# A retention and mixture-of-experts kernel: the first expert's rows turned set by set into four banks, and two output tiles run together by kind of product

## The chip, the cores and the metric

The kernel runs on one core of a Trainium2 chip. The metric is the time of one execution on the device in microseconds (us); 409.28 us is the median of three executions before the change.

## The reference

Retention with a decaying state for 4 batches of 8 heads over 768 steps, then a mixture of 8 experts over the 3072 rows that come out, each row going to the one expert with the largest logit.

```python
for t in range(S):                        # attention part, B=4 H=8 S=768 D=64
    state = gamma * state + k[t] v[t]^T
    y[t] = scale * q[t] state
x = y.transpose(0, 2, 1, 3).reshape(3072, 512)
logits = normalized(x) @ normalized(expert_emb).T / tau
expert_idx = argmax(logits, axis=1)       # gate_w: softmax probability of that expert
for e in range(8):
    mask = expert_idx == e
    h = np.maximum(x[mask] @ w1[e], 0.0)  # 512 -> 1024
    out[mask] = gate_w[mask, None] * (h @ w2[e])
```

## The kernel before

**Two parts.** The attention runs as 12 blocks of 256 steps (the loop over `m`, 0 to 11). Each block gives two banks of PSUM, `py0` and `py1`, which ScalarE copies to `yT` (function `take`, lines 460 and 463). From `yT` come the rows, written to the table `xd` in memory, and the logits: TensorE multiplies (`logits_products`, line 488), VectorE turns the result (`logits_rows`), a further product sums it (`sums`, line 506), VectorE picks the expert (`choose`), and `count` (lines 533 to 537) with `ranks` gives every row its slot in a table, into which GpSimd scatters the row's number (`place`). This goes by groups of blocks; the last two groups are block 10 with its predecessor (`done` in the last pass) and block 11 alone (`g`).

**Experts.** Weights come in pieces of 512 KB. Every piece is split in a high part (`whi`, a rounded copy by ScalarE, line 219) and a low part (`wlo`, the difference, VectorE, line 224), and so are the activations (`xh` and `xl`, `hh` and `hl`). A product of two such numbers is three TensorE products: high by high, high weight by low activation, low weight by high activation. One output tile of the first layer (`first_layer`, line 237) is 4 steps over the inner dimension (`kt`) with three products each, 12 in all, summed in one PSUM bank. There are eight such tiles (`ft`); `hidden` takes a finished one through the ReLU (ScalarE, line 243) and makes the low part (VectorE, line 246).

**The first expert starts early.** 288 of its rows are gathered into `xge` while the attention's last blocks still run, as two sets of 128 rows and one of 32 (`EROWS`). TensorE transposes them (`turn_rows`, line 613): one bank for each `kt`, its three sets one behind the other. ScalarE casts each bank to `xh` (line 620) and VectorE subtracts to `xl` (line 621). The first expert's products are then handed out by `run(n)`, which issues the next n products, so that the logits' steps of the last block stand between them.

**Order.** Instructions of each engine execute in the order in which the program issues them, since the schedule is set by hand for all five engines. PSUM has eight banks. Four (`b0` to `b3`) are taken in turn by `pt_()`; accumulators of the experts go through `py0`, `py1`, `pst0`, `pst1`, `b0`, `b1` (`acc_()`). A bank's next user waits until its last reader is done. So the first two accumulators of the first expert, `py0` and `py1`, wait for `take` of block 11.

Of the kernel before, what the change touches and what calls it, by code (L numbers as in the profile page):

```python
# [11 lines left out]
F32 = mybir.dt.float32  # L12
# [5 lines left out]
ALU = mybir.AluOpType  # L18
# [6 lines left out]
P = 128  # L25
# [9 lines left out]
KT = DM // P  # L35
# [70 lines left out]
def retention_moe(ctx: ExitStack, tc: tile.TileContext, q, k, v, emb, tau, w1, w2, const, const16, out):  # L106
# [45 lines left out]
    def bank(tag, bufs=1):  # L152
        return ps_.tile([P, 512], F32, name=tag, bufs=bufs)
# [5 lines left out]
    def pt_():  # L159
        npt[0] += 1  # L160
        return bank(turn_of[npt[0] % len(turn_of)])
# [291 lines left out]
    def intra(m, u):  # L453
        for j in range(KT):
            for a in range(2):
                y_product(m, u, j, a, vs[m][:, u, 2 * j + a], pms[a, u][:, j])
# [72 lines left out]
    def count(g):  # L529
        r = span(g)  # L530
        nb = r.stop - r.start
        pr = pt_()
        nc.tensor.matmul(pr[:, :nb * NE], ones, cum[:, r.start:r.start + 1].broadcast_to([P, nb, NE]), start=True,
                         stop=False, skip_group_check=True)
        nc.tensor.matmul(pr[:, :nb * NE], tri, oh[:, r], start=False, stop=False, skip_group_check=True)
        for i in range(1, nb):
            nc.tensor.matmul(pr[:, i * NE:nb * NE], ones, oh[:, r.start:r.stop - i], start=False, stop=(i == nb - 1),
                             skip_group_check=True)
        return pr
# [9 lines left out]
    def ranks(g, pr):  # L549
        r = span(g)  # L550
        nb = r.stop - r.start
        rs = ap_.tile([P, nb, NE], F32, name="rs", bufs=1)
        nc.vector.tensor_tensor(out=rs, in0=pr[:, :nb * NE].rearrange("p (c e) -> p c e", e=NE), in1=oh[:, r], op=ALU.mult)
        yield
        nc.vector.tensor_reduce(out=rank[:, r], in_=rs, axis=AX.X, op=ALU.add)
        yield
        nc.vector.scalar_tensor_tensor(out=sloti[:, r], in0=wmn[:, r], scalar=16.0 * STRIDE, in1=rank[:, r],  # L557
                                       op0=ALU.mult, op1=ALU.add)
        yield
# [13 lines left out]
    def run_all(*gs):  # L573
        gs = list(gs)
        while gs:
            gs = [g for g in gs if next(g, gs) is not gs]
# [30 lines left out]
        tokens(P, 0, slice(0, 3))  # L607
        return i

    def turn_rows(xr, jn, kt, ps=None):  # L610
        ps = pt_() if ps is None else ps
        for c, (j, n) in enumerate(jn):
            nc.tensor.transpose(ps[:, c * P:c * P + n], xr[:n, j, kt * P:(kt + 1) * P], ident[:n, :n])
        return ps

    def rows_T(xr, jn, kt, at, ps=None):

        ps = turn_rows(xr, jn, kt) if ps is None else ps
        w = at.stop - at.start
        nc.scalar.copy(out=xh0[:, kt, at], in_=ps[:, :w])  # L620
        nc.vector.tensor_tensor(out=xl0[:, kt, at], in0=ps[:, :w], in1=xh0[:, kt, at].bitcast(F32), op=ALU.subtract)  # L621

    def expert_emb():
        em = ap_.tile([NE, DM], F32, name="parts")
# [136 lines left out]
    for m in range(NM):  # L761
        nxt = m + 1 < NM
        done = last_of.get(m - 1)
        if waiting is not None:
            pr = count(waiting)
            run_all(ranks(waiting, pr))
            if span(waiting).stop == NBE:
                pad()
            ready += range(span(waiting).start, span(waiting).stop)
        py_of(m)  # L770
        if m == NM - 2:
            first = [split_cast(), split_cast()]

        for u in range(2):
            o = masks(scores(m, u), u)
            if u == 0:
                i = o[0]
        n = 2 if m < 7 else 3 if m < 8 else 4
        if m == NM - 2:
            place(ready)  # L780
            ready = []
        if m == 0:
            for j in (*load_q(2), load_k(2)):
                after(j, i)
            nc.sync.dma_start(out=cst2, in_=const[:, _C1:])
            nc.sync.dma_start(out=tri, in_=const16)

        if m + 2 < NM:
            for s in range(2):
                after(scale_k(m + 2, s), i)  # L790
            for s in range(2):
                after(scale_q(m + 2, s), i)
        if m == 2:
            nc.gpsimd.tensor_copy(out=zt[:, :, :2].bitcast(I32), in_=C("ids").rearrange("p (n o) -> p n o", o=2))
        place(ready[:n])
        del ready[:n]
        if m == NM - 3:
            load_piece()
            load_piece()
        if m == NM - 2:  # L800
            early_slots()
            gathered = early_gather()
        if m and m + 3 < NM:
            for j in load_q(m + 3):
                after(j, i)
        if m == 0:
            state(0)
            state_copy(0)
            state_sums(0)
            intra(0, 0)  # L810
            intra(0, 1)
            transpose_k(1, 0)
            i = transpose_k(1, 1)
            after(load_v(2), i)
            inter(0)
            transpose_q(1, 0)
            i = transpose_q(1, 1)
            for j in (*load_q(3), load_k(3), load_v(3)):
                after(j, i)
            state(1)  # L820
            state_copy(1)
            state_sums(1)
        else:
            inter(m)
            if nxt:
                i = state(m + 1)
                state_copy(m + 1)
                if m + 3 < NM:
                    after(load_k(m + 3), i)
            if m == 2:  # L830
                after(nc.sync.dma_start(
                    out=tbl.rearrange("(e s) c -> e (s c)", e=NE)[:, :FILL * SW].rearrange("e (p x) -> e p x", p=P // NE),
                    in_=none), i)
            for i in () if m < 3 else (0, 1, 2) if m == 3 else (m - 1,):
                logits_rows(i, logits_products(i))
            if nxt:
                state_sums(m + 1)
                spread_v(m, 1, nc.vector.tensor_copy)
                transpose_k(m + 1, 0)
                transpose_q(m + 1, 0)  # L840
                i = transpose_q(m + 1, 1)
                if m + 3 < NM:
                    after(load_v(m + 3), i)
                transpose_k(m + 1, 1)
                if m == NM - 2:
                    spread_v(m + 1, 0)
                if m == NM - 3:
                    z = sums(done)
                    run_all(choose(done, z))
                    run_all(add_counts(done))  # L850
                rows(m - 1, gathered if m == NM - 2 else None)
                if m == NM - 2:
                    for low in first:
                        low()
                    load_piece(gathered)
                    load_piece(gathered)
                if done is not None and m != NM - 3:
                    z = sums(done)
                    run_all(choose(done, z))
                    run_all(add_counts(done))  # L860
                intra(m, 0)
                intra(m, 1)
            else:
                intra(m, 0)
                z = sums(done)
                run_all(choose(done, z))
                run_all(add_counts(done))
                for low in lows:
                    low()
                intra(m, 1)  # L870
                pr = count(done)
                ps = [turn_rows(xge, EROWS, kt, bank(f"pst{kt}")) for kt in range(2)]
                run_all(ranks(done, pr))
                place(range(span(done).start, span(done).stop))
        waiting = done
        take(m)
        if m < NM - 2:
            spread_v(m + 1, 0)
        if m == NM - 2:
            spread_v(m + 1, 1)  # L880
            lows = [split_cast(), split_cast()]
        if m < 3:
            next(emb_steps)
        if m == NM - 1:
            for kt in range(KT):
                rows_T(xge, EROWS, kt, slice(0, EARLY), ps[kt] if kt < 2 else None)

        for _ in range(LOADS.count(m)):
            load_piece()
# [6 lines left out]
    held = []  # L896

    def products():
        for ft in range(FT):
            acc = acc_()  # L900
            yield from first_layer(0, ft, acc, xh0, xl0, early)
            hidden(ft, acc, hh0, hl0, early, held if ft < 2 else None)

    todo = products()

# [7 lines left out]
        nc.sync.dma_start(out=tb[:, e], in_=tbl[ds(expert[e] * STRIDE, NG * P), :2 + NE].rearrange("(j p) o -> p j o", p=P))  # L913

    m, g = NM - 1, len(GROUPS) - 1
    pl = logits_products(m)
    logits_rows(m, pl)
    rows(m - 1)
    load_piece()
    load_piece()  # L920
    run(11)
    low = split_cast()
    z = sums(g)
    run_all(choose(g, z))
# [435 lines left out]
```

## Time and profile before

| what | value |
|---|---|
| median of 3 executions | 409.28 us (408.39 to 411.97) |
| the profiled execution | 409.33 us, of which the span from first to last instruction is 407.6 us |
| TensorE busy | 392.3 us, 96% of the span |
| VectorE, ScalarE, GpSimd busy | 254.2 us, 213.5 us, 154.8 us |
| hardware DMA queue q1 | 74.60 MB, 64.5% of the 16 engines' span |
| mean granted TensorE clock | 0.986 of full speed |

Busy shares are means over the whole span. The place of the change is a stretch of some 10 us, from about 121 to 131 us, between the last attention block and the first expert; there the order of the engines' instructions and what each waits for are to be read, not the shares.

### The profile page before, as it was taken

Reading aid. Unit: us, or ns where it says so; the run is one execution under the profiler, and the core shown is the slowest. Engines: PE = TensorE matmul, PEld = TensorE weight load, DVE = VectorE, ACT = ScalarE, POOL = GpSimd, SP = SyncE. Lnnn points to the kernel's source line nnn. Section 1 sums busy time; section 2 is a strip of 40 time slices with the busy share of each in tenths; the row PEclk is TensorE's granted clock in tenths of the full one; section 3 lists DMA queues with packets and bytes.
Section 4 is the critical chain, followed back from the end, with each engine's and each line's share of the span. In section 5 each row is a group of like instructions: output and inputs, shape, how many; then the busy total and the mean of one; then the engine's idle time right before and its main releaser. Section 6 shows DMA issues by size and latency. Waiting matters only on the chain.

```text
span 407.6 us, 9526 instructions
## 1 busy us (share of the span) xinstructions
PE 392.3 (96%) x3646; PEld 359.1 (88%) x3646; DVE 254.2 (62%) x539; ACT 213.5 (52%) x378; POOL 154.8 (38%) x170
## 2 busy tenths in 40 slices
PE   7999999999899999999999999999999999999993
PEld 3998788878687998899999999999889889999972
DVE  5496877767489847871963676396266465586400
ACT  4565566545484627543745644565475365563410
POOL 2666477676333270701631330261274062000040
PEclk9999999999799999999999999999999999999997
DMA  8998979888437978879596896888969958934121
GB/s 233 266 291 255 270 218 261 238 220 245 112 81 189 277 233 198 282 222 276 187 297 166 254 301 197 233 280 248 257 242 329 206 183 247 247 127 126 32 98 53
DMA packets 88479, 88.39 MB, mean 217 GB/s; under 512 B 10808, under 2 KB 67000, under 8 KB 88424
## 3 DMA queue, kind: packets, MB, share of 16 engines
q1 hardware_dynamic: 83176, 74.60, 64.5%
q0 software_dynamic: 5072, 13.03, 9.4%
q8 instruction: 30, 0.49, 0.5%
q14 instruction: 25, 0.20, 0.1%
q10 hardware_dynamic: 176, 0.07, 0.1%
HBM read 65.01 MB, written 18.79 MB: 206 GB/s over the span
## 4 chain that ended last, share of the span: by engine, by line
PE 76%; DVE 6%; issue 6%; DMA 5%; SPq 4%; POOL 1%; ACT 1%; POOLq 0%; DVEq 0%; ACTq 0%
PE pst L237 11%; PE b L237 9%; PE py L237 8%; PE py L1030 8%; PE b L1030 6%; PE pst L1030 6%; PE py L444 5%; PE b L381 5%; PE b L1078 4%; PE py L1078 4%; PE pst L415 2%; SPq L1042 2%; PE b L350 2%; DMA tbl<-parts 2%; DVE x L468 2%
## 5 line engine op out<-in xcount | busy, mean ns | idle before, releaser
L224 DVE TENSOR_TENSOR wlo<-raw,whi 128x1024 fp32r<-128x1024 f32 x64 | 77.8, 1219 | 21.0 <-ACT whi L219 13.6
L1060 POOL DMA_INDIRECT out_dram<-og,si x28 | 30.4, 1086 | 125.1 <-ACT og L1053 88.7
L219 ACT CAST whi<-raw 128x1024 fp32r<-128x1024 f32 x64 | 66.2, 1044 | 2.1 <-DMA raw<-in_moe_w_dram 2.1
L1011 DVE STREAM_TRANSPOSE xt<-xg 128x384 f32<-128x384 f32 (+1 forms) x28 | 15.7, 579 | 34.1 <-DMA xg<-xs 33.9
L596 POOL DMA_INDIRECT xr<-xd,gi x24 | 29.9, 1244 | 17.2 <-ACT sq L278 9.9
L401 DVE TENSOR_TENSOR pm<-b,mask 128x512 f32<-128x512 f32 x48 | 29.8, 681 | 9.1 <-PE b L381 9.1
L344 POOL TENSOR_TENSOR hl<-wlo,cst 128x512 f32<-128x512 f32 x22 | 22.7, 1051 | 32.9 <-DMA wlo<-in_k_dram 20.9
L237 PE MATMUL pst<-xl,whi 128*128 128x380 f32 (+7 forms) x96 | 32.1, 335 | 0.2 <-issue 0.2
L237 PE MATMUL pst<-xh,whi 128*128 128x380 f32 (+7 forms) x96 | 32.0, 334 | 0.0
L237 PE MATMUL pst<-xh,wlo 128*128 128x380 f32 (+7 forms) x96 | 32.0, 333 | 0.0
L566 POOL DMA_INDIRECT tbl<-zt,sloti x24 | 24.4, 1018 | 19.2 <-DVE sloti L557 8.9
L381 PE MATMUL b<-qT,kT 64*128 64x128 f32 x384 | 27.9, 283 | 2.9 <-issue 2.0
L1012 ACT CAST xh<-xt 128x408 fp32r<-128x408 f32 (+6 forms) x28 | 14.3, 510 | 28.4 <-DVE xt L1011 27.4
L381 PEld LDWEIGHTS b<-qT,kT 64*128 64x128 f32 x384 | 24.0, 187 | 5.6 <-issue 3.8
L237 PE MATMUL py<-xl,whi 128*128 128x288 f32 (+7 forms) x80 | 26.3, 328 | 0.5 <-DVE xl L621 0.5
L237 PE MATMUL b<-xh,whi 128*128 128x408 f32 (+7 forms) x80 | 26.7, 334 | 0.0
L237 PE MATMUL b<-xl,whi 128*128 128x408 f32 (+7 forms) x80 | 26.7, 333 | 0.0
L237 PE MATMUL b<-xh,wlo 128*128 128x408 f32 (+7 forms) x80 | 26.6, 332 | 0.0
L237 PE MATMUL py<-xh,whi 128*128 128x288 f32 (+7 forms) x80 | 26.3, 329 | 0.0
L237 PE MATMUL py<-xh,wlo 128*128 128x288 f32 (+7 forms) x80 | 26.2, 328 | 0.0
L444 PE MATMUL py<-pm,vs 128*64 128x128 f32 x384 | 24.3, 277 | 0.3 <-DVE vs L394 0.3
L243 ACT ACTIVATE hh<-pst 128x380 fp32r<-128x380 f32 (+7 forms) x24 | 11.6, 484 | 23.8 <-PE pst L237 23.1
(222 smaller groups left out, 1036.5 us busy)
## 6 DMA issues: line engine op xcount, KB each, us to landing
raw<-in_moe_w_dram SPq DMA_DIRECT2D x60, 512.0 KB
whi<-in_q_dram SPq DMA_DIRECT2D x24, 256.0 KB
xd<-x SPq DMA_DIRECT2D x48, 128.0 KB
wlo<-in_k_dram SPq DMA_DIRECT2D x11, 512.0 KB
xs<-xr SPq DMA_DIRECT2D x6, 768.0 KB
whi<-in_v_dram SPq DMA_DIRECT2D x6, 512.0 KB
wlo<-in_v_dram SPq DMA_DIRECT2D x6, 512.0 KB
xg<-xs SPq DMA_DIRECT2D x16, 192.0 KB
```

What stands on the lines that cost most here:

```text
L219: nc.scalar.copy(out=hv, in_=rv)
L224: eng.tensor_tensor(out=lv, in0=rv, in1=hv.bitcast(F32), op=ALU.subtract)
L237: nc.tensor.matmul(acc[:, :w], a[:, f], x[:, kt, cols], start=(n == 0), stop=(n == 3 * KT - 1))
L344: return eng.tensor_tensor(out=ks_r[:, m % 3, s, h], in0=kin[m % 3][:, h, s], in1=w[:, h], op=ALU.mult)
L381: nc.tensor.matmul(psc[a][:, j], kTs[m][a * D:(a + 1) * D, j, u].rearrange("p s c -> p (s c)"), q_cols(m, a, j, u), start=True, stop=True, ...
L401: o.append(nc.vector.tensor_tensor(out=pm, in0=psc[a], in1=w, op=ALU.mult))
L444: nc.tensor.matmul(pys[m][u][o * D:(o + 1) * D, j], lhsT, rhs, start=first, stop=True, skip_group_check=True)
L566: i = nc.gpsimd.indirect_dma_start(out=tbl[:, :], out_offset=bass.IndirectOffsetOnAxis(ap=sloti[:, n:n + 1], axis=0), in_=zt[:, n], in_off ...
L596: return nc.gpsimd.indirect_dma_start(out=xr[:n, j, :], out_offset=None, in_=xd[:rows_, :], in_offset=bass.IndirectOffsetOnAxis(ap=gi[:n, ...
L1030: nc.tensor.matmul(acc[:, :c], a[:, f], x[:, kt, :c], start=(n == 0), stop=(n == 3 * FT - 1))
L1060: i = nc.gpsimd.indirect_dma_start(out=out[:, :], out_offset=bass.IndirectOffsetOnAxis(ap=si[:n, e, j:j + 1], axis=0), in_=og[:n, j, :], i ...
L1078: nc.tensor.matmul(acc[:s, :], x[:, kt, at], a, start=(n == 0), stop=(n == 3 * FT - 1))
```

## The change

- The rows are turned set by set: the first 128 rows into all four banks (`pst0`, `pst1` and two of `b0` to `b3`), then the second 128, then the last 32. The transposes now stand ahead of `count`, where before they stood behind it.
- The four casts to `xh` (`rows_high`) are issued ahead of `take` of block 11, where before they came behind it. The four subtractions (`rows_low`) come ahead of the second of two weight splits, of `ranks` and of `place`.
- The first two output tiles open together, in two accumulators: for each kind of product (high by high, then low activations, then low weights) and each `kt`, one product for each of the two tiles.
- The first 12 products stand ahead of `logits_products` of block 11, 6 more ahead of the next split and `sums`, where before 11 came between these two and none ahead.

```diff
-    def turn_rows(xr, jn, kt, ps=None):
-        ps = pt_() if ps is None else ps
+    def turn_rows(xr, jn, ps):
         for c, (j, n) in enumerate(jn):
-            nc.tensor.transpose(ps[:, c * P:c * P + n], xr[:n, j, kt * P:(kt + 1) * P], ident[:n, :n])
-        return ps
-
-    def rows_T(xr, jn, kt, at, ps=None):
-
-        ps = turn_rows(xr, jn, kt) if ps is None else ps
-        w = at.stop - at.start
-        nc.scalar.copy(out=xh0[:, kt, at], in_=ps[:, :w])
-        nc.vector.tensor_tensor(out=xl0[:, kt, at], in0=ps[:, :w], in1=xh0[:, kt, at].bitcast(F32), op=ALU.subtract)
+            for kt in range(KT):
+                nc.tensor.transpose(ps[kt][:, c * P:c * P + n], xr[:n, j, kt * P:(kt + 1) * P], ident[:n, :n])
+
+    def rows_high(kt, at, ps):
+        nc.scalar.copy(out=xh0[:, kt, at], in_=ps[:, at])
+
+    def rows_low(kt, at, ps):
+        nc.vector.tensor_tensor(out=xl0[:, kt, at], in0=ps[:, at], in1=xh0[:, kt, at].bitcast(F32), op=ALU.subtract)
...
                 run_all(add_counts(done))
-                for low in lows:
-                    low()
+                lows.pop(0)()
                 intra(m, 1)
+                ps = [bank(f"pst{kt}") for kt in range(2)] + [pt_(), pt_()]
+                turn_rows(xge, EROWS, ps)
                 pr = count(done)
-                ps = [turn_rows(xge, EROWS, kt, bank(f"pst{kt}")) for kt in range(2)]
-                run_all(ranks(done, pr))
-                place(range(span(done).start, span(done).stop))
+                for kt in range(KT):
+                    rows_high(kt, slice(0, EARLY), ps[kt])
         waiting = done
         take(m)
...
         if m == NM - 1:
             for kt in range(KT):
-                rows_T(xge, EROWS, kt, slice(0, EARLY), ps[kt] if kt < 2 else None)
+                rows_low(kt, slice(0, EARLY), ps[kt])
+            lows.pop(0)()
+            run_all(ranks(done, pr))
+            place(range(span(done).start, span(done).stop))
...
     def products():
-        for ft in range(FT):
+        accs = [acc_(), acc_()]
+        for i in range(3):
+            for kt in range(KT):
+                x = xl0 if i == 1 else xh0
+                for ft, acc in enumerate(accs):
+                    nc.tensor.matmul(acc[:, :EARLY], piece[kt][i // 2][:, ft * P:(ft + 1) * P], x[:, kt, early],
+                                     start=(i + kt == 0), stop=(i == 2 and kt == KT - 1))
+                    yield
+        for ft, acc in enumerate(accs):
+            hidden(ft, acc, hh0, hl0, early, held)
+        for ft in range(2, FT):
             acc = acc_()
             yield from first_layer(0, ft, acc, xh0, xl0, early)
-            hidden(ft, acc, hh0, hl0, early, held if ft < 2 else None)
+            hidden(ft, acc, hh0, hl0, early)
...
+    run(12)
     pl = logits_products(m)
     logits_rows(m, pl)
     rows(m - 1)
     load_piece()
     load_piece()
-    run(11)
+    run(6)
     low = split_cast()
```

ScalarE, around the end of block 11, as one piece of the difference (`xh` is the high part of the turned rows, the `py` banks with numbers 2082 and 2083 are the two results of block 11, which here free the banks `py0` and `py1`; `hh` is the first layer's output):

```order
 L219 CAST whi<-raw 128x1024 x2
+L616 CAST xh<-pst_2166 128x288
+L616 CAST xh<-pst_2167 128x288
+L616 CAST xh<-b_2168 128x288
+L616 CAST xh<-b_2169 128x288
 L460 COPY yT<-py_2082 128x4x128
 L463 COPY yT<-py_2083 64x4x128 x2
-L620 CAST xh<-pst_2173 128x288
-L620 CAST xh<-pst_2177 128x288
-L620 CAST xh<-b_2205 128x288
-L620 CAST xh<-b_2211 128x288
```

The three copies that free `py0` and `py1` stood ahead of the four casts and now stand behind them.

TensorE before, from the end of the count of the last but one group to the first products of the first expert (`py_2237` is its first accumulator):

```order
L537 MATMUL b_2167<-oh,ones 128x8
L613 MATMUL pst_2173<-ident,xge 128x128 x2
L613 MATMUL pst_2173<-ident,xge 128x32
L613 MATMUL pst_2177<-ident,xge 128x128 x2
L613 MATMUL pst_2177<-ident,xge 128x32
L613 MATMUL b_2205<-ident,xge 128x128 x2
L613 MATMUL b_2205<-ident,xge 128x32
L613 MATMUL b_2211<-ident,xge 128x128 x2
L613 MATMUL b_2211<-ident,xge 128x32
L488 MATMUL b_2219<-yT,enT 32x256 x4
L237 MATMUL py_2237<-xh,whi 128x288
L237 MATMUL py_2237<-xl,whi 128x288
```

TensorE now, from the last set's transposes to the first products (`py_2219` lies in bank `py0`, `py_2220` in bank `py1`; two rows of the count are in front of the first product):

```order
L613 MATMUL pst_2166<-ident,xge 128x32
L613 MATMUL pst_2167<-ident,xge 128x32
L613 MATMUL b_2168<-ident,xge 128x32
L613 MATMUL b_2169<-ident,xge 128x32
...
L537 MATMUL b_2182<-oh,ones 128x8
L905 MATMUL py_2219<-xh,whi 128x288
L905 MATMUL py_2220<-xh,whi 128x288
L905 MATMUL py_2219<-xh,whi 128x288
L905 MATMUL py_2220<-xh,whi 128x288
```

The short transposes, each bank's last, stand together at the end; the second product of the first expert already needs the second bank, and the logits' products have moved from ahead of the first product to behind the twelfth.

## Rows read from the trace of the kernel before

**Rows 1.** The page: the span, and TensorE's busy time.
```profile
span 407.6 us, 9526 instructions
PE 392.3 (96%) x3646; PEld 359.1 (88%) x3646; DVE 254.2 (62%) x539; ACT 213.5 (52%) x378; POOL 154.8 (38%) x170
```

**Rows 2.** TensorE's waits from 125 us on: who waited, for what, us, times, longest.
```profile
PE py L237 <- DVE xl L621: 0.5, 1, 0.5
```

**Rows 3.** TensorE's timeline, 120.9 to 126.5 us: start, us, instruction, count, idle before.
```profile
120.92 1.09 PE L444 MATMUL py<-pm,vs 128*64 128x128 f32 x16
121.94 0.19 PE L533 MATMUL b<-cum,ones 128*128 128x32 f16 x1
122.20 0.18 PE L535 MATMUL b<-oh,tri 128*128 128x32 f16 x1
...
122.30 1.14 PE L613 MATMUL pst<-ident,xge 128*128 128x128 f32 x6
123.37 1.16 PE L613 MATMUL b<-ident,xge 128*128 128x128 f32 x6
124.45 0.64 PE L488 MATMUL b<-yT,enT 128*32 128x256 f32 x8
125.02 0.40 PE L237 MATMUL py<-xh,whi 128*128 128x288 f32 x1
125.93 0.40 PE L237 MATMUL py<-xl,whi 128*128 128x288 f32 x1 [0.51 <-DVE xl L621]
126.17 0.29 PE L237 MATMUL py<-xh,wlo 128*128 128x288 f32 x1
126.30 0.29 PE L237 MATMUL py<-xh,whi 128*128 128x288 f32 x1
```

**Rows 4.** ScalarE's timeline, 121.2 to 125 us.
```profile
121.19 0.58 ACT L460 COPY yT<-py 128x512 f32<-128x512 f32 x1
122.06 1.17 ACT L463 COPY yT<-py 64x512 f32<-64x512 f32 x2 [0.29 <-PE py L444]
123.25 0.70 ACT L620 CAST xh<-pst 128x288 fp32r<-128x288 f32 x2
124.01 0.94 ACT L620 CAST xh<-b 128x288 fp32r<-128x288 f32 x2
```

**Rows 5.** VectorE's timeline, 122.6 to 126.3 us.
```profile
122.63 2.36 DVE L224 TENSOR_TENSOR wlo<-raw,whi 128x1024 fp32r<-128x1024 f32 x2
...
125.42 0.81 DVE L621 TENSOR_TENSOR xl<-pst,xh 128x288 fp32r<-128x288 f32 x2
```

**Rows 6.** TensorE's timeline, two later places.
```profile
130.55 0.18 PE L533 MATMUL b<-cum,ones 128*128 128x16 f16 x1
...
147.94 0.29 PE L1030 MATMUL b<-hh,wlo 128*128 128x288 f32 x1
148.29 0.63 PE L1100 MATMUL b<-ident,xr 128*128 128x128 f32 x4
```

**Rows 7.** GpSimd's timeline: a gather of the early rows, and that of the late.
```profile
114.98 1.52 POOL L596 DMA_INDIRECT xge<-xd,tb  x1 [0.30 <-issue]
...
143.90 1.16 POOL L596 DMA_INDIRECT xr<-xd,tb  x1 [4.59 <-DMA tb<-tbl]
```

**Rows 8.** SyncE's timeline: the rows' write that waits for the early gathers.
```profile
119.84 2.54 SPq L475 DMA_DIRECT2D xd<-x  x4
```

**Rows 9.** Stretches of 2 us: length, busy us of PE, PEld, DVE, ACT, POOL, granted clock, DMA.
```profile
102.00:104.00 2.00, 0.93 (x8) 0.63 (x7) 0.02 (x1) 0.59 (x1) 1.25 (x2) 1.00 0.96 243
106.00:108.00 2.00, 2.00 (x36) 1.78 (x36) 1.97 (x5) 1.94 (x3) 1.68 (x2) 0.60 0.33 89
112.00:114.00 2.00, 2.00 (x14) 2.00 (x13) 1.94 (x6) 1.15 (x3) 1.45 (x2) 0.69 0.00 0
124.00:126.00 2.00, 1.49 (x13) 0.66 (x13) 1.93 (x6) 0.80 (x2) 0.21 (x1) 1.00 1.00 286
```

**Rows 10.** The same, at the end of the program.
```profile
400.50:401.00 0.50, 0.33 (x2) 0.00 (x0) 0.00 (x0) 0.14 (x1) 0.00 (x0) 1.00 0.14 33
403.00:404.00 1.00, 0.00 (x0) 0.00 (x0) 0.00 (x0) 0.00 (x0) 0.17 (x1) 0.68 0.21 49
```

## The prediction, made before the change was run

> **What bounds the kernel now.** I read the page first: TensorE is busy for 392.3 of 407.6 us [rows 1], so a shift of its queue should reach the end. The list of waits then says whether it does: behind 125 us TensorE waits once, 0.5 us for the low part of the turned rows [rows 2]. From there to the last product its queue is full, so time lost or won between 121 and 131 us arrives at the end nearly whole. I therefore read the timelines of TensorE, ScalarE and VectorE there and compared them with the order of their instructions before and now.
>
> In that stretch the reader should see this. The last attention products begin at 120.92 and end their issue at 121.94. The count's second product comes 0.26 us behind its first, where some 0.05 would do: it waits for VectorE, about 0.2 us. Twelve transposes fill 122.30 to 124.45, 0.54 us for each bank. The logits' products take to 125.02. The first product of the expert starts at 125.02 and the second at 125.93, while later ones follow each other by 0.13 us: 0.78 us are lost to the wait for `xl` [rows 3]. On ScalarE the copies of block 11 run from 121.19 to 123.23, beside the transposes, and the four casts follow as the transposes end [rows 4]. This is the point to keep: the copies are hidden under the transposes, and the banks that they free are free before anybody wants them.
>
> **The change part by part.** *Removed.* The transposes stand ahead of the count, whose 0.2 us of waiting is then covered. The low parts come fourfold later in the queue than the high ones, and VectorE makes them ahead of the second weight split (a pair of splits took 2.36 us [rows 5]); so the 0.78 us go too. Together 1.0 us is taken away.
>
> *Added, on ScalarE.* The four casts are now queued ahead of the three copies of block 11. ScalarE executes in order, so the copies wait until the casts are done, and the casts wait for the transposes. The transposes can start at about 121.95 and need 2.15 us [rows 3], so their issue ends at 124.1. Each bank's last set comes in the last four, which are short (I take 0.15 us each, an estimate from 0.54 us for two long and one short); the first bank is whole at about 123.65, and a cast began about 0.1 us behind its bank before. First cast: 123.8. Casts follow each other by 0.35 us (two in 0.70 [rows 4]), four make 1.4, so the copy of the first bank starts at 125.2 and ends at 125.8 (0.58), and the pair of copies of the second bank ends at 126.95 (1.17 [rows 4]). Before, they ended at 121.8 and 123.2.
>
> *Added, on TensorE.* The first product writes `py0` and the second `py1`. The count after the transposes ends at about 124.25. The first product starts at 125.82, when `py0` is read: 1.57 us of standing. The second wants `py1`, free at 126.95; with the 0.06 us that the restart behind a wait took in the rows (`xl` done, product started), it starts at 127.02: 1.20 us after the first in place of 0.13, so 1.07 us more. Behind it in the queue stand all other products, and the logits' products too, which need nothing but the copies. Added: 2.64 us. Net of the 1.0 us removed: **+1.65 us**. A second way to the same: the second product starts 1.09 us later than before (127.02 against 125.93), and 0.57 us of logits' products [rows 3] still stand behind it that were done before; 1.66.
>
> *Hidden.* The low parts start at about 124.3 behind one split and end at 125.8, the second split at 127; the ninth product, the first to want a low part, comes at about 128 and the seventeenth, the first on a low weight, later still. Neither waits. The four scatters of the last but one group start some 2 us later, and GpSimd had nothing to do then. These edits cost nothing; if `xl` were late by more than 2 us, that would show as the old wait.
>
> *Moved: the count of block 11 and what hangs on it.* It stands behind 39 products now, 32 before; 7 products are 0.93 us. So it moves from 130.55 [rows 6] to about 133.2, some 2.6 us, and with it the sort, SyncE's queue behind the sort's result, and the gather of the first expert's late rows at 143.90 [rows 7]. VectorE skips one interleaved step there, so I put this chain at +2.2 us. Does TensorE meet it? SyncE's write that waits for the early gathers started at 119.84 [rows 8], 3.3 us behind the end of the last of them on GpSimd (116.50 [rows 7]); that is the longest that a gather can have taken to land. The late gather ended its issue at 145.06; with 3.3 us it lands at 148.4, and TensorE turns these rows at 148.29, 0.2 us later than the pace of the products ahead of it would put it [rows 6]. So it is just in time now, and with the chain 0.5 us later than TensorE it is late: between 0 and 0.5 us, I take **+0.3 us**.
>
> *The clock.* Nothing before shows TensorE standing at just this place for so long, so this cost is bounded by the nearest rows. From 102 to 104 us TensorE was busy 0.93 of 2 us; the granted clock fell at about 106.4 (0.60 in 106 to 108) to the 1.2 GHz level and rose at about 113.2 (0.69 in 112 to 114): 6.8 us [rows 9]. At the end TensorE stops at 400.83 and the clock falls at about 403.4 [rows 10]. After the shorter stop at 125 us, 0.51 us of 2, the clock stayed at 1.00, the 2.4 GHz level [rows 9]. The new stop, 2.6 us with one product in it, is like the first two. So I expect the clock to fall at about 127 us or soon after. The cost is between 0 (no fall) and 3.4 us (half speed for 6.8 us). The work behind the stop is of full-width products without a gap, unlike that of 106 to 113 us, which may bring the clock back sooner; I take half, **+1.7 us**.
>
> The Trainium skill, page "TensorE: Matmul & The Clock Gate", section "A second HAM failure mode: psum-queue depth-cycling", tells of a kernel whose TensorE stood briefly between groups of products while it went through PSUM banks, and whose clock swung between its two levels for it. By that rule this change, which makes TensorE wait for two banks, gives 413.0; if it did not hold here, 411.3. The trace is divided: the short stop at 125 us brought no fall, the two longer ones did.
>
> *Sum.* 1.65 + 0.3 + 1.7 = 3.65 us onto the profiled execution's 409.33 (span 407.6), which lies 0.05 us from the median of 409.28: **413.0 us**.
>
> **The rivals.** *The stop without the fall:* the sum is 1.95 us, 411.3 us. For it: the work after the stop is dense, and the stop is broken by one product. Against it: both longer stops of the trace ended in a fall.
>
> *Not slower:* the copies of block 11 are done, or nearly so, when the high products begin, and only the removed waits count. It decides at about 125 us: if the second pair of copies ends before that, TensorE goes on from its count without a stop, and the 1.0 us removed gives 408.4; if it ends at 125.9, the two cancel at 409.3. For it: ScalarE had nothing to do for 0.29 us at 122 us and the copies need only 1.8 us. Against it: in the order of the changed kernel they stand behind four casts that can't start before 123.6, and nothing lets ScalarE overtake. It would need casts that start a microsecond earlier than the transposes allow.
>
> *The change doesn't do what it says:* if the transposes over four banks in turn took longer than in one (each changes its bank), the casts begin later still; at 0.05 us more for each of twelve that is 0.6 us more, 413.6 with the fall. That is inside the range.
>
> *More than that:* a fall of the clock that lasts its 6.8 us and a weight load that comes late in addition, since SyncE's rows and pieces 6 and 7 move by over 2 us: 415 us or more.
>
> **How the numbers follow.** Stop and fall 0.50, at 413.0 (its own range 411.8 to 414.7, a fall of nearly no length to the full one); stop alone 0.32, at 411.3 (410.6 to 411.8); not slower 0.13 (408.4 to 409.9); over 414.9, 0.05. The range leaves out the last two: 410.4 to 414.9. A measurement of this kernel can tell about 1% from no change, which is 4.1 us: slower means over 413.4. About 0.42 of the first case lies there (0.21), and the last case (0.05): 0.26. Faster by over 1% would be below 405.2, and nothing reaches that: 0.02. The rest, 0.72, is within 1%.
>
> **What would show it.** Right: on ScalarE four casts from about 123.8 and the three copies behind them, ending near 127; on TensorE the first product at about 125.8 and the second at about 127.0, both put down to ScalarE; no wait for `xl` any more; a granted clock near 0.5 for some us from about 127 or soon after; the late rows' transposes waiting for their gather by a few tenths. The step on the clock is wrong if the granted clock stays 1.00 between 124 and 136 us; then 411.3 holds. The whole is wrong if the second product starts before 126 us, or if a later stretch of TensorE's queue, full until now, turns out to have slack that gives the microseconds back.

## The result and the profile after

| | before | after |
|---|---|---|
| median of 20 executions each | 408.56 us (404.97 to 412.45) | 411.66 us (409.65 to 415.89) |
| ratio after to before | | 1.0077, 95% interval 1.0055 to 1.0098 |
| profiled execution, span | 409.33 us, 407.6 us | 409.97 us, 408.2 us |
| its mean granted clock | 0.986 | 0.994 |

The kernel became slower by 3.1 us in the median, inside the range of 410.4 to 414.9 us and within 1%. The two profiled executions differ by 0.64 us only. That is no contradiction: in that of before the clock also fell inside the attention, at 106 us [rows 9], and in that of after it did not (1.00 in 106 to 108 us). What the change does is therefore read from times counted from the start of the last sixteen attention products (120.92 before, 118.00 now), not from the spans:

| us behind that start | first product | second product | count of block 11 | late rows turned | second expert, 2nd tile | end |
|---|---|---|---|---|---|---|
| before | 4.10 | 5.01 | 9.63 | 27.37 | 46.68 | 286.7 |
| after | 4.18 | 5.38 | 13.03 | 30.01 | 50.19 | 290.2 |

From the second expert's second tile on both take 240.0 us. All of the difference arises ahead of it.

The page of after; its two lines answer to [rows 1], with TensorE as busy as before:

```profile
span 408.2 us, 9527 instructions
PE 391.5 (96%) x3646; PEld 358.8 (88%) x3646; DVE 254.3 (62%) x539; ACT 213.3 (52%) x378; POOL 149.7 (37%) x170
```

TensorE's waits of after between 118 and 180 us. Where [rows 2] had one wait for `xl`, there are two for ScalarE's copies:

```profile
PE py L905 <- ACT yT L460: 1.5, 1, 1.5
PE py L905 <- ACT yT L463: 0.8, 1, 0.8
PE pst L237 <- DVE xl L1030: 0.6, 2, 0.3
```

TensorE's timeline of after (start, us, instruction, count, idle before), against [rows 3]:

```profile
119.03 0.44 PE L613 MATMUL pst<-ident,xge 128*128 128x128 f32 x2
...
120.20 0.28 PE L613 MATMUL b<-ident,xge 32*128 32x32 f32 x2
120.41 0.19 PE L533 MATMUL b<-cum,ones 128*128 128x32 f16 x1
...
122.18 0.40 PE L905 MATMUL py<-xh,whi 128*128 128x288 f32 x1 [1.49 <-ACT yT L460]
123.38 2.05 PE L905 MATMUL py<-xh,whi 128*128 128x288 f32 x7 [0.80 <-ACT yT L463]
125.22 1.16 PE L905 MATMUL py<-xl,whi 128*128 128x288 f32 x4
126.31 0.71 PE L488 MATMUL b<-yT,enT 128*32 128x256 f32 x8
```

Three things stand here. The two products are 1.20 us apart, and nothing waits for `xl` any more. The transposes take 1.38 us (119.03 to 120.41), where before they took 2.15. And the eleven products from the second to the twelfth take 2.93 us (123.38 to 126.31), twice the 0.133 us each of full speed.

ScalarE's timeline of after, against [rows 4]: casts, then copies, without a gap.

```profile
120.33 0.70 ACT L616 CAST xh<-pst 128x288 fp32r<-128x288 f32 x2 [1.91 <-PE pst L613]
120.92 0.72 ACT L616 CAST xh<-b 128x288 fp32r<-128x288 f32 x2
121.50 0.63 ACT L460 COPY yT<-py 128x512 f32<-128x512 f32 x1
122.15 1.17 ACT L463 COPY yT<-py 64x512 f32<-64x512 f32 x2
```

VectorE's timeline of after, against [rows 5]: the low parts stand between the two splits and are done at 122.4, ahead of the first product that wants one.

```profile
119.70 1.23 DVE L224 TENSOR_TENSOR wlo<-raw,whi 128x1024 fp32r<-128x1024 f32 x1
120.85 0.82 DVE L619 TENSOR_TENSOR xl<-pst,xh 128x288 fp32r<-128x288 f32 x2
121.58 0.81 DVE L619 TENSOR_TENSOR xl<-b,xh 128x288 fp32r<-128x288 f32 x2
122.31 1.22 DVE L224 TENSOR_TENSOR wlo<-raw,whi 128x1024 fp32r<-128x1024 f32 x1
```

Stretches of 2 us of after, columns as in [rows 9]; the granted clock is the number ahead of the last two. It goes from full to 0.50 and back in some 3.4 us:

```profile
120.00:122.00 2.00, 0.69 (x11) 0.51 (x9) 2.00 (x5) 1.67 (x5) 0.00 (x0) 1.00 0.83 205
122.00:124.00 2.00, 1.02 (x3) 0.81 (x4) 1.93 (x6) 1.29 (x3) 0.00 (x0) 0.78 1.04 346
124.00:126.00 2.00, 2.00 (x10) 2.00 (x9) 0.04 (x1) 1.05 (x1) 1.37 (x2) 0.50 0.33 119
126.00:128.00 2.00, 2.00 (x21) 1.12 (x23) 0.90 (x2) 0.00 (x0) 1.65 (x2) 0.87 0.05 6
```

Later places of after, TensorE's timeline, against [rows 6]: the count, and the late rows (no wait).

```profile
131.03 0.18 PE L533 MATMUL b<-cum,ones 128*128 128x16 f16 x1
...
148.01 0.60 PE L1112 MATMUL b<-ident,xr 128*128 128x128 f32 x4
```

### The profile page after: what moved, and what is told of

Read it like the earlier page. It is cut to its first block, busy times and chain, and to the rows that moved or that the text cites. A ratio compares the mean times of both kernels' runs of the same rounds, so it can differ in the third digit from the quotient of the medians.

```text
span 408.2 us, 9527 instructions
## 1 busy us (share of the span) xinstructions
PE 391.5 (96%) x3646; PEld 358.8 (88%) x3646; DVE 254.3 (62%) x539; ACT 213.3 (52%) x378; POOL 149.7 (37%) x170
## 3 DMA queue, kind: packets, MB, share of 16 engines
q0 software_dynamic: 5072, 13.03, 9.5%
## 4 chain that ended last, share of the span: by engine, by line
PE 68%; DVE 8%; DMA 7%; issue 7%; SPq 4%; ACT 2%; POOL 2%; POOLq 0%; DVEq 0%; ACTq 0%
PE pst L237 10%; PE b L237 8%; PE py L1042 7%; PE py L237 7%; PE b L1042 5%; PE py L444 5%; PE b L381 4%; PE pst L1042 4%; PE b L1090 4%; PE py L1090 4%; SPq L1054 2%; PE pst L415 2%; DVE x L468 2%; PE b L350 2%; DVE vs L394 1%
## 5 line engine op out<-in xcount | busy, mean ns | idle before, releaser
L1072 POOL DMA_INDIRECT out_dram<-og,si x28 | 29.3, 1046 | 126.0 <-ACT og L1065 76.5
L263 POOL TENSOR_TENSOR r<-r,half 128x4 f32<-128x4 f32 (+1 forms) x9 | 8.9, 991 | 43.7 <-DVE r L262 43.7
L237 PE MATMUL py<-xh,whi 128*128 128x360 f32 (+7 forms) x72 | 23.9, 331 | 0.0
L237 PE MATMUL py<-xl,whi 128*128 128x360 f32 (+7 forms) x72 | 23.8, 330 | 0.0
```

What stands on the lines that cost most here:

```text
L237: nc.tensor.matmul(acc[:, :w], a[:, f], x[:, kt, cols], start=(n == 0), stop=(n == 3 * KT - 1))
L1072: i = nc.gpsimd.indirect_dma_start(out=out[:, :], out_offset=bass.IndirectOffsetOnAxis(ap=si[:n, e, j:j + 1], axis=0), in_=og[:n, j, :], i ...
```

## The experiments

Runs told together ran on one chip beside the kernel before. That kernel took 401.7 us (first group), 409.3 us (second), 402.0 us (third) and 402.2 us (the last run), so ratios are compared and times are not. Theory: ScalarE's order is the cause, since the copies that free `py0` and `py1` stand behind four casts. Rivals: the fall of the clock is the cost, whatever the stop; or the later count and what hangs on it.

**First group: the order alone, and its parts.**

*e1, the change with the copies first:*

```diff
                 pr = count(done)
-                for kt in range(KT):
-                    rows_high(kt, slice(0, EARLY), ps[kt])
         waiting = done
         take(m)
+        if m == NM - 1:
+            for kt in range(KT):
+                rows_high(kt, slice(0, EARLY), ps[kt])
```

> The changed kernel with only ScalarE's order put back: the three copies of block 11 ahead of the four casts. Theory (the copies behind the casts hold the banks py0 and py1, and TensorE stands for them): both stops of TensorE, 1.5 and 0.8 us in the changed kernel's trace, are gone, the clock doesn't fall there, and the time is 0.3 to 1.5 us under the kernel before (ratio 0.996 to 0.999), which is 3.4 to 4.6 us under the change. Rival (it is the pairing of two tiles, the moved logits' products and the later count that cost): the time stays 2 us or more over the kernel before (ratio 1.005 or more).

Measured: ratio 1.0009 (0.9984 to 1.0034). The stops are gone, the granted clock is 1.00 from 112 to 124 us, and the first product comes 2.85 us behind the start of the last attention products. So the order is needed for the loss. The gain that was expected does not appear. TensorE's waits of e1 between 112 and 180 us say where it went:

```profile
PE b L237 <- DVE rs L553: 1.0, 1, 1.0
PE pst L237 <- DVE xl L1031: 0.6, 2, 0.3
```

The first wait is for VectorE's last reader of the bank, the ranks of block 11 (L553). VectorE's timeline of e1 shows it queued behind a low part, which waited for ScalarE's ReLU:

```profile
123.89 0.46 DVE L246 SCALAR_TENSOR_TENSOR hl<-pst,hh 128x288 fp32r<-128x288 f32 x1 [1.29 <-ACT hh L243]
124.27 0.16 DVE L553 TENSOR_TENSOR rs<-b,oh 128x16 f32<-128x16 f32 x1
```

And ScalarE's timeline of e1 shows the ReLU queued behind a weight cast whose DMA was late:

```profile
121.83 1.05 ACT L219 CAST whi<-raw 128x1024 fp32r<-128x1024 f32 x1 [5.74 <-DMA raw<-in_moe_w_dram]
122.79 0.70 ACT L243 ACTIVATE hh<-py 128x288 fp32r<-128x288 f32 x2
```

TensorE, a microsecond early, met a chain that starts at a transfer; that this chain doesn't move with it is read from this one trace.

*e2, the kernel before with only the four casts ahead of the copies:*

```diff
                 ps = [turn_rows(xge, EROWS, kt, bank(f"pst{kt}")) for kt in range(2)]
+                ps += [turn_rows(xge, EROWS, kt) for kt in (2, 3)]
                 run_all(ranks(done, pr))
                 place(range(span(done).start, span(done).stop))
+                for kt in range(KT):
+                    nc.scalar.copy(out=xh0[:, kt, :EARLY], in_=ps[kt][:, :EARLY])
...
-                rows_T(xge, EROWS, kt, slice(0, EARLY), ps[kt] if kt < 2 else None)
+                nc.vector.tensor_tensor(out=xl0[:, kt, :EARLY], in0=ps[kt][:, :EARLY], in1=xh0[:, kt, :EARLY].bitcast(F32), op=ALU.subtract)
```

> The kernel before with only ScalarE's order changed: the four casts ahead of the three copies, everything else (transposes bank by bank behind the count, one tile at a time, logits' products first) as it was. Theory: TensorE stands some 2.3 us ahead of the logits' products, the wait for the low parts (0.8 us) goes, net 1.5 us, and in about half of the executions the clock falls behind it for another 1.5 us: 1.5 to 3.0 us over the kernel before (ratio 1.004 to 1.007). Rival (pairing and moved logits): no change, ratio 0.999 to 1.001.

Measured: ratio 1.0074 (1.0048 to 1.0099), 3.0 us: about as much as the whole change, by this order alone, and a little over the 1.007 that was expected. TensorE's waits of e2 between 113 and 180 us; the second, among the transposes, is for the gather of the early rows, which the edit doesn't touch:

```profile
PE b L488 <- ACT yT L463: 2.2, 1, 2.2
PE pst L613 <- DMA xge<-xd,tb: 0.5, 2, 0.3
```

The first is the stop that the theory names. The granted clock behind it, in stretches of 2 us, fell as in the change:

```profile
120.00:122.00 2.00, 2.00 (x14) 1.59 (x15) 1.31 (x3) 0.00 (x0) 1.60 (x2) 0.64 1.01 299
122.00:124.00 2.00, 2.00 (x16) 1.68 (x16) 0.46 (x2) 1.04 (x1) 0.97 (x1) 0.51 0.81 274
```

*e3, the change with the first two tiles one after the other,* so that the second bank is wanted twelve products later:

```diff
-        for i in range(3):
-            for kt in range(KT):
-                x = xl0 if i == 1 else xh0
-                for ft, acc in enumerate(accs):
+        for ft, acc in enumerate(accs):
+            for i in range(3):
+                for kt in range(KT):
+                    x = xl0 if i == 1 else xh0
```

> The changed kernel with the two first tiles one behind the other, each by kind of product, in place of together. Theory: the first tile needs only py0, so the second stop (0.8 us, for py1) goes and the first (1.5 us) stays; the time is 0.8 us under the change, and up to 2.3 us where the shorter stop also spares the fall of the clock: ratio to the kernel before 1.002 to 1.006. Rival (the second stop costs nothing, because the chain of the second expert's rows ends later anyway): as the change, ratio 1.007 to 1.008.

Measured: ratio 1.0036 (1.0009 to 1.0064), 1.5 us. One stop of 1.5 us is left, and the clock still fell (0.50 in 118 to 120 us). By the middle values the first stop and the fall are worth about half of what e2 shows; the intervals of the two overlap, so what the second stop costs is not settled.

*e4, the change with sixteen products on a spare bank, which compute nothing, in the two stops:*

```diff
+        fill = bank(turn_of[(npt[0] + 1) % 4])
+        def filler(n):
+            for _ in range(n):
+                nc.tensor.matmul(fill[:, :EARLY], piece[0][0][:, :P], piece[0][0][:, :EARLY], start=True, stop=True)
+        filler(10)
...
+                    if i + kt + ft == 0:
+                        filler(6)
```

> The changed kernel with 16 added products into an unused bank, whose results nobody reads, where TensorE stands: 10 ahead of the first product and 6 between the first and the second (0.13 us each, 1.3 and 0.8 us). Theory (stop and fall of the clock are two costs): the stop stays, the granted clock stays 1.00 behind it, and the time is 0.8 to 1.5 us under the change, ratio to the kernel before 1.003 to 1.006. Rival (the fall costs nothing that the stop and the later chain don't cost anyway): as the change, ratio 1.007 to 1.008.

Measured: ratio 1.0050 (1.0018 to 1.0083). The clock stays up; stretches of 2 us of e4:

```profile
116.00:118.00 2.00, 2.00 (x20) 1.78 (x19) 1.88 (x5) 1.73 (x5) 0.00 (x0) 1.00 0.36 79
118.00:120.00 2.00, 1.93 (x13) 1.64 (x13) 1.84 (x5) 1.23 (x3) 0.00 (x0) 1.00 0.95 198
120.00:122.00 2.00, 2.00 (x19) 1.42 (x19) 0.31 (x1) 0.00 (x0) 1.51 (x2) 1.00 0.93 279
```

The added products fit into the stops: the first two products of the expert come 4.48 and 5.68 us behind the start, in the change on a like chip (c2, below) 4.52 and 5.71. From the second of them to the count e4 takes 6.31 us, after 7.65 and c2 7.75: the fall costs 1.3 to 1.4 us there, on one trace each. But the second expert's second tile comes at 50.55 us, no earlier than the 50.19 of after, and TensorE's waits of e4 name VectorE:

```profile
PE pst L1051 <- DVE hl L246: 0.9, 1, 0.9
PE pst L237 <- DVE xl L1039: 0.6, 2, 0.3
```

So the rival "the clock is the cost, whatever the stop" falls: without the fall there is still a loss. How large the clock's share of it is, the interval leaves open: from the 1.0060 of the change on a like chip (c2, below) to the low end here would be 1.7 us, to the middle 0.4.

**Second group: the change, its repair tried further, and the count.**

*c0, the kernel before, for its trace on this chip:*

> The kernel before, unchanged, for a trace beside the others of these runs. All theories: from the last 16 attention products of block 11 to the count of block 11 9.6 us, to the second output tile of the second expert 46 to 47 us, and 240.0 us from there to the end of the span.

Measured: one execution, 408.15 us; 9.62 us to the count, as in the first trace of before, 46.50 us to the second expert's second tile, and 240.0 us from there to the end.

*c1, the change unaltered:*

> The change, unchanged, beside the others of these runs. All theories: ratio to the kernel before 1.005 to 1.010; two stops of TensorE of 1.5 and 0.8 us, put down to the copies of block 11; the granted clock falls behind them for about 3.4 us in most executions.

Measured: ratio 1.0045 (1.0017 to 1.0074), just under the range that was expected; the stops are 1.5 and 0.8 us again, the granted clock fell behind them (0.50 in 128 to 130 us), and the count comes at 13.15 us.

*e5, e1 with the count put back by seven products (`run(14)` for `run(21)`) and the weight cast behind them:*

```diff
-    low = split_cast()
...
-    run(21)
+    run(14)
+    low = split_cast()
```

> The changed kernel with ScalarE's copies ahead of the casts, the count of block 11 behind 32 products again in place of 39, and the high cast of weight piece 4 moved on ScalarE behind the ReLU of the first two tiles. Theory (what the pairing and the set by set turning give was eaten, with the copies first, by a wait for VectorE behind a weight cast that waited for its piece, and by the later count): no wait of TensorE of 0.5 us or more up to the second expert, and the time is 0.4 to 1.6 us under the kernel before, ratio 0.996 to 0.999. Rival (the rows of the second expert set the time however early the first expert starts): ratio 1.000 to 1.002.

Measured: ratio 1.0044 (1.0010 to 1.0079), slower than before; the middle lies over both ranges that were expected. The count comes early (8.62 us), and the wait for the ranks (e1) is gone, but TensorE waits 0.9 us for a low part of the second layer and 0.9 us by "issue". ScalarE's ReLU of a tile whose products were complete at about 130.7 starts at 135.03, and the two waits by "issue" (the engine waited for nothing that the profile shows) lie at 134.3 to 135.8. What held ScalarE is not in the trace; this stays open.

*e6, the change with only the count put back by seven products:*

```diff
-    run(21)
+    run(14)
```

> The changed kernel with the count of block 11 behind 32 products again in place of 39, nothing else. Theory (the later count puts up to 0.9 us on the rows of the second expert, for which TensorE waits 0.6 us in the changed kernel's trace): 0.4 to 1.0 us under the change, ratio 1.004 to 1.007 where the change has 1.0077. Rival (TensorE's stops set the time alone): as the change, within 0.2 us.

Measured: ratio 1.0057 (1.0018 to 1.0096), no better than c1 beside it. The intervals alone are too wide to exclude a gain of 0.9 us, but the traces show none: the second expert's second tile comes at 49.36 us, in c1 at 49.21. And e1, which keeps the later count, is not slower than before. So the rival of the later count falls.

**Third group: the gains, one by one.**

*e7, the kernel before with only the transposes set by set* (`turn_rows` with its two loops exchanged, all four banks taken at once; casts, copies, count and products as before):

```diff
-        for c, (j, n) in enumerate(jn):
-            nc.tensor.transpose(ps[:, c * P:c * P + n], xr[:n, j, kt * P:(kt + 1) * P], ident[:n, :n])
+        for c, (j, n) in enumerate(jn):
+            for kt in range(KT):
+                nc.tensor.transpose(ps[kt][:, c * P:c * P + n], xr[:n, j, kt * P:(kt + 1) * P], ident[:n, :n])
```

> The kernel before, with one part of the change alone: the twelve transposes go set by set into four banks; order of the casts, the copies, the count and the products as before. Theory (the queue behind is full): in the changed kernel these transposes took 1.38 us where before they took 2.15, so the logits' products start about 0.7 us earlier and the ratio is 0.998 to 0.999. Rival (the next wait eats it): the first product on a low part waits for VectorE's subtraction, which doesn't move, so its 0.5 us of waiting grow to about 1.2 and the ratio is 1.000.

Measured: ratio 0.9994 (0.9972 to 1.0017), the rival's 1.000. TensorE's timeline of e7:

```profile
115.55 0.42 PE L613 MATMUL pst<-ident,xge 128*128 128x128 f32 x2
...
116.24 0.38 PE L613 MATMUL b<-ident,xge 128*128 128x128 f32 x2
116.55 0.30 PE L613 MATMUL pst<-ident,xge 32*128 32x32 f32 x2
116.70 0.28 PE L613 MATMUL b<-ident,xge 32*128 32x32 f32 x2
116.91 0.64 PE L488 MATMUL b<-yT,enT 128*32 128x256 f32 x8
117.48 0.40 PE L237 MATMUL py<-xh,whi 128*128 128x288 f32 x1
119.18 0.40 PE L237 MATMUL py<-xl,whi 128*128 128x288 f32 x1 [1.30 <-DVE xl L619]
```

The transposes take 1.36 us, so their gain of 0.79 us belongs to their order and not to anything else in the change. Two things are new in that order: each transpose goes to another bank than the one before, and the four short ones (32 rows, `32*128` in the rows) stand together. The single starts tell these apart. TensorE's timeline of before, the second to the fourth transpose, each in a window of its own:

```profile
122.44 0.27 PE L613 MATMUL pst<-ident,xge 128*128 128x128 f32 x1
122.65 0.24 PE L613 MATMUL pst<-ident,xge 32*128 32x32 f32 x1
122.82 0.33 PE L613 MATMUL pst<-ident,xge 128*128 128x128 f32 x1
```

The first two long ones start 0.145 us apart there, both into one bank (122.30 [rows 3] and 122.44), and 0.144 us apart in e7, into two banks. A short one starts 0.204 us behind a long one there, in the same bank, and 0.203 us in e7, in another. So the bank makes no difference that these starts show; the change between long and short does. In e7 the next start comes 0.109 us behind a long one when a long one follows, and 0.062 us behind a short one when a short one follows. In before it comes 0.204 us behind a long one when a short one follows, 0.175 us behind the short one, and 0.164 us behind the long one after that. Together that is 0.26 us more for each time there and back. Before has three more of these than e7, which makes the 0.79 us. No run changed the banks alone.

And the wait for `xl`, 0.51 us before [rows 3], is 1.30 now: longer by just 0.79. The count comes at 9.62 us, as before.

*e8, e1 with the logits' products ahead of the first product again and 32 products ahead of the count, as in the kernel before:*

```diff
-    run(12)
     pl = logits_products(m)
...
-    run(6)
+    run(11)
```

> The changed kernel with the copies of block 11 ahead of the casts, and with the logits' products again ahead of the first product, 11 products between them and the sums, so 32 ahead of the count as before. What is left of the change: the transposes set by set and ahead of the first count, the low parts ahead of the second split, the two tiles together. Theory (time won in this stretch reaches the end): no stop, 0.77 us of transposes, 0.2 and 0.78 us of waits gone: 1.5 to 1.8 us faster than before, ratio 0.9955 to 0.9965. Rival (VectorE's and ScalarE's steps towards the second layer and the second expert's rows set the time next): the count comes 1.5 us earlier by the trace, the second expert's rows do not, ratio 0.999 to 1.001.

Measured: ratio 1.0004 (0.9981 to 1.0027), again the rival's. But its trace is not the rival's: the count comes at 10.15 us, 0.5 us later than before, where the rival had it 1.5 us earlier (0.3 us of this is a wait of the transposes for the early rows' gather). TensorE's timeline of e8 at the sums, which now stand still where before they did not:

```profile
118.36 0.26 PE L506 MATMUL b<-parts,cst 128*32 128x16 f32 x8 [1.47 <-DVE parts L496]
```

VectorE's timeline of e8 shows why: it is busy without a gap from 114.75 on, and the logits' transpose (L496) has its turn when low parts, split and ranks are through.

```profile
114.75 0.82 DVE L619 TENSOR_TENSOR xl<-pst,xh 128x288 fp32r<-128x288 f32 x2 [0.48 <-ACT xh L616]
115.49 0.81 DVE L619 TENSOR_TENSOR xl<-b,xh 128x288 fp32r<-128x288 f32 x2
116.22 1.21 DVE L224 TENSOR_TENSOR wlo<-raw,whi 128x1024 fp32r<-128x1024 f32 x1
...
117.87 0.44 DVE L496 STREAM_TRANSPOSE parts<-b 128x256 f32<-128x256 f32 x1
```

*e9, e1 once more:*

> The changed kernel with only the copies of block 11 put ahead of the four casts, once more, on another chip and beside the two others. Theory (the order of ScalarE is the whole cause of the loss): ratio 0.998 to 1.002 as the first time (1.0009). Rival (the first result belonged to a chip on which the clock hardly falls at all): ratio 1.004 to 1.006, like the changed kernel.

Measured: ratio 0.9991 (0.9964 to 1.0018). On another chip too, the change with the copies first is not slower than before.

**Last, c2, the change once more,** on a chip like that of the first and third groups:

> The changed kernel itself, once more. Theory (stop and fall of the clock are its own, whatever the chip does elsewhere): ratio 1.005 to 1.009. Rival (on a chip that holds its clock high elsewhere the loss is the stop alone, 1 us or less): ratio 1.000 to 1.003.

Measured: ratio 1.0060 (1.0039 to 1.0082), with stops of 1.5 and 0.8 us and a granted clock of 0.67 in 118 to 120 and 0.50 in 120 to 122 us, behind them. The loss does not hang on the chip. No version that was run beats the kernel before.

## Why the prediction was right, and where not

- **ScalarE's order as the cause: right, and shown** from both sides. The order alone makes the loss (e2, 1.0074); without it the change costs nothing that these runs can tell (e1 and e9, 1.0009 and 0.9991, each to about 1 us). The two products 1.20 us apart were forecast to the hundredth.
- **The length of the transposes: mis-sized.** The step "need 2.15 us" took the old order's time for the new one; it is 1.38 us, and e7 shows that the order does this, by fewer changes between long and short transposes. The rival had the opposite sign (0.6 us more, for a change of bank each time); the change of bank cost nothing that the traces show. So the casts start 2.33 us behind the start of the last attention products and not 2.9, and the second product comes at 5.38 us and not 6.10. With the 0.57 us of logits' products behind it, the net of the stops is 5.38 - 5.01 + 0.57 = 0.94 us in place of 1.65.
- **The fall of the clock: right in kind, near in size.** It came, lasted some 3.4 us where the nearest row had 6.8 [rows 9], and stretched the eleven products to 2.93 us from 1.47: 1.5 us by the count, where 1.7 was forecast. The Trainium skill, page "TensorE: Matmul & The Clock Gate", section "A second HAM failure mode: psum-queue depth-cycling", tells of a clock that swings between its two levels where TensorE stands briefly, again and again, while it goes through PSUM banks; the trace agrees in that the clock fell behind the stops (0.50 in 124 to 126 us), but it fell once and did not swing. And e4, which kept 1.00, stayed at 1.0050, so how much of this term reaches the end was not settled.
- **The count and the late rows: wrong place.** The +0.3 us for the late rows did not come; they are turned at 148.01 us without a wait. The profiled execution lost 0.9 us at the second expert's rows instead (20.18 us from the late rows to its second tile, 19.31 before), but c1 took 19.09 and c2 19.04, so this is no steady term. e6 shows that the later count itself costs nothing that can be measured. So this term, put at 0.3, measured 0.
- **The step that failed in principle:** "time lost or won between 121 and 131 us arrives at the end nearly whole". It held for the time lost (2.47 us at the count, without the seven products that moved ahead of it, and 2.64 us at the late rows), not for time won. In e7 0.79 us, in e8 the stops and both old waits were taken away, and the wait for VectorE grew instead: from 0.5 to 1.3 us for `xl`, to 1.47 us for the sums. In e1 the first product came 1.25 us earlier than before and the count not at all (9.55 against 9.63 us; seven more products, 0.93 us, stand ahead of it). VectorE, busy 1.93 of 2 us there before [rows 9], has no more room than TensorE. The credit of 1.0 us for removed waits was right only because a longer stop lay in the same place.
- **The sum.** By the count it is 0.94 + 1.5 = 2.4 us of the 13.03 - 9.63 - 0.93 = 2.47 that the trace shows. The first comparison gives 3.1 us, c1 and c2 by their ratios 1.8 and 2.4 us; 3.65 was forecast. All three terms were too large, by 0.7, 0.2 and 0.3 us. That 3.1 lies so near 3.65 is in part luck: the steps, corrected, give 2.4, and what the profiled execution lost beyond that, 0.9 us at the second expert's rows, no step had, and c1 and c2 don't show it. Nor does the time speak for the fall against the rival of the stop alone: 411.66 us lies in that rival's range (410.6 to 411.8), and 1.8 and 2.4 us are nearer to its 1.95 than to 3.65. That the clock fell is known from the traces alone.

Open remains what exactly carries the loss to the end when the clock does not fall (e4): the waits for VectorE at the second layer and the second expert name it, but no run took them away. Open too is what held ScalarE in e5. And no trace of before was taken on a chip like those of the first and third groups: from the start of the last attention products to the end e1 and e9 take 288.0 and 288.2 us, the two traces of before 286.7 and 286.5 on slower chips, so whether the change with the copies first loses a microsecond in this stretch, which its ratio does not show, is not known.

## What to carry to other kernels

Before a cast or copy is moved ahead on an in-order engine, list what it is moved past and which PSUM banks those instructions free: here two banks stood behind four casts, which cost 2 to 3 us, and the rest of the change, run without that, won nothing. A full queue on the busiest engine says that losses there arrive, not that gains do; for a gain, read what the next engine could deliver earlier. Opening two accumulators at once asks for both banks at once.

## What the hardware showed that was not expected

- Twelve transposes, eight of 128 rows and four of 32, took 2.15 us as long, long, short four times over, and 1.36 to 1.38 us with the four short ones at the end (e7 alone, and the change). From long to short the next start came 0.20 us later, whether in the same bank or another, against 0.11 us from long to long in e7 and 0.06 from short to short.
- Standing still for 1.5 and 0.8 us with one product between (the change), for 2.2 us at once (e2), or for 1.5 us alone (e3) brought the granted clock to 0.50 or 0.51 each time; sixteen empty products in the same place kept it at 1.00 (e4).
- That half clock lasted some 3.4 us, and taking it away (e4) moved the count by 1.3 to 1.4 us, measured from the second product, and the end by less than these runs can tell apart.
